# First MLP: the first product of six token tiles as Strassen's seven block products, in pairs

## The chip, the cores and the metric

The kernel runs on one core of one Trainium2 chip. The metric is the device time of one execution in microseconds (us). Three runs of the kernel before gave 1450.2, 1450.25 and 1452.52; their median is 1450.25.

TensorE (PE) does the matrix products, VectorE (DVE) and ScalarE (ACT) everything elementwise. SyncE (SP) issues nearly all DMAs, one after the other. In the trace each engine's instructions run in the order in which the built program has them, with waits on semaphores for the others.

## The reference

Three stages in a row, all in float32. `B, H, S, D = 8, 8, 576, 64`, so there are 4608 tokens of 512 numbers.

```python
kv  = einsum('bhsd,bhse->bhde', k, v)            # linear attention
out = einsum('bhsd,bhde->bhse', q, kv)
out = out / sqrt(mean(out*out, -1) + 1e-6) * g_norm
x   = out.transpose(0, 2, 1, 3).reshape(4608, 512)

h = x @ w_in                                     # first MLP, 512 -> 2048 -> 512
g = s * maximum(h, 0)**2 + b
y = g @ w_out

z = maximum(maximum(y @ w1, y @ w2), y @ w3)     # second MLP, 512 -> 768 -> 512
result = z @ w_out2
```

The two weights of the first MLP and the four of the second arrive as float64 bits, and the kernel turns them into float32 itself.

## The kernel before

**Precision.** Every operand of a product is split into a rounded part (hi) and the rest (lo); a product is three matmuls, hi*hi, hi*lo and lo*hi. `hilo` makes the split with one ACT copy and one DVE subtraction (L92, L93).

**Tiles.** The tokens form 9 tiles of 512. Features lie on the partitions. For one tile the first MLP takes 16 blocks `f` of 128 hidden features. `u1` (L345) makes `h`: 4 parts of the 512 inputs, 3 matmuls each, 12 matmuls of 512 columns. `u1_end` turns `h` into the gates: ACT takes the relu (L354), DVE squares and scales it (L355), ACT adds `b` and rounds it to `gh` (L356), DVE forms the rest `gl` (L357). `u2` (L368) multiplies the gates by `w_out` into four PSUM banks, 12 matmuls again, two blocks behind `u1`. A tile is so 384 matmuls, and each has 12 others between the end of an `h` and the use of its gates.

**Order.** Tiles 0 and 1 share a head in three blocks of hidden features, in which the weights arrive and are turned into float32 (L107 to L112). Tiles 2 to 6 follow one by one, and tiles 7 and 8 share two blocks. Beside tile `t - 1` runs the attention of tile `t`, item by item (an item is two heads of 256 or 320 tokens): `s2` splits `q` on ACT and DVE, `s3` (L266) multiplies it with `kv` on PE, ACT squares the result and scales it (L268, L273), `hilo` splits the square, `s4` (L303, L304) averages it on PE, then ACT takes logarithm, exponential and square (L306 to L308), and DVE corrects and multiplies (L309, L310, L313). `put_x` splits the result into the tile that `u1` reads. From 257 us on a tile takes 96 us, attention included.

**Second MLP.** It runs over pairs of tiles (`SUPERS`) and uses Strassen's scheme in Winograd's form: `combine` forms 7 blocks out of four weight blocks, `tok_steps` 7 out of four token blocks, and `v1` (L508) makes 7 block products where 8 would be the plain way. Its weights are prepared beside the first MLP (`Plain` beside tiles 2 to 6, `combine` and `split_out` beside the last two) and pass through DRAM.

**What decides the order.** The kernel is written as one stream of operations with lists of side work, of which a share is put out after each step of the main work. A scheduler then places the instructions of each engine by the stream's order and its own estimate of when each is ready. The trace has them in that order.

Of the kernel before, what the change touches and what calls it, by code (L numbers as in the profile page):

```python
# [8 lines left out]
F32 = mybir.dt.float32  # L9
# [15 lines left out]
def fused_kernel(ctx, tc, qt, kv, kvr, g_norm, w_in, w_out, s, b, w1, w2, w3, w_out2, out):  # L25
# [17 lines left out]
    XO = 192  # L43
    LIMITS = [CUTS[0]] + [(i + 1) * TW for i in range(NTILE)]

    FA = KF // 2
# [5 lines left out]

    mlp1, attn, low = (ctx.enter_context(ExitStack()) for _ in range(3))
# [3 lines left out]
    wpa = pool("wpa", 2 * FA, st=low, side="right")  # L57
    rawp = pool("rawp", 2, st=mlp1)
    wtp = pool("wtp", 2, st=mlp1)
    wt1 = pool("wt1", 2, st=mlp1)  # L60
    xp = pool("xp", 2, st=mlp1)
    gp = pool("gp", 2, st=mlp1)
    stp = pool("stp", 4, st=mlp1)
    gp1 = pool("gp1", 1, st=mlp1)
    wpb = pool("wpb", 2 * (KF - FA), st=mlp1)
    ps_y = pool("ps_y", 1, PSUM, st=mlp1)
    ps_h = pool("ps_h", 2, PSUM, st=mlp1)
    ps_a = pool("ps_a", 2, PSUM, st=mlp1)
# [7 lines left out]
    start = [wpb.tile([P, NP + 2, P], F32, tag="w", name=f"start{i}") for i in range(EARLY)]  # L76
# [5 lines left out]
    y_dr = [dram.tile([P, KD, TW], F32, name=f"y_dr{t}") for t in range(NTILE)]  # L82
    NQ = KM // 2 * 3
    HW = DM // 2
    wf_dr = [[dram.tile([P, DM], F32, name=f"wf_dr{j}_{m}") for m in range(KM)] for j in range(4)]
# [3 lines left out]
    dma = nc.sync.dma_start  # L89

# [5 lines left out]
    def w_load(src):  # L96
        raw = rawp.tile([P, 2 * DM], U32, tag="raw", name="raw")
        dma(out=raw, in_=src)
        return raw

    def w_float(raw):
        words = raw.rearrange("p (c z) -> p c z", z=2)
        low, high = words[:, :, 0], words[:, :, 1]
        ta = wt1.tile([P, DM], U32, tag="ta", name="ta")
        tb = wtp.tile([P, DM], U32, tag="tb", name="tb")
        af, bf = ta.bitcast(F32), tb.bitcast(F32)
# [6 lines left out]
        return bf  # L113

    def w_parts(bf, nm, f):
        t = (wpa if f < FA else wpb).tile([P, 2, DM], F32R, tag="w", name=nm)
        with tc.high_priority(60):
            hilo(t[:, 0, :], t[:, 1, :], bf)
        return t

    class Weights:
# [6 lines left out]
        def load(self, cnt):  # L128
            while self.loaded < min(cnt, len(self.need)):
                self.raw[self.loaded] = w_load(self.need[self.loaded][0])  # L130
                self.loaded += 1

        def to(self, cnt):
            cnt = min(cnt, len(self.need))
            while self.done < cnt:
                self.load(self.half + 3)
                if self.half < len(self.need):
                    self.f32[self.half] = w_float(self.raw.pop(self.half))
                    self.half += 1
                if self.done < self.half - 1 or self.half == len(self.need):  # L140
                    _, d, key = self.need[self.done]
                    d[key] = w_parts(self.f32.pop(self.done), f"w{self.done}", key)
# [11 lines left out]
    def load_kv(bb, p):  # L154
# [8 lines left out]
        t = wpa.tile([P, NC, 2, P], F32, tag="w", name="kv")  # L163
# [695 lines left out]
```

## Time and profile before

| | |
|---|---|
| runs, us | 1450.2, 1450.25, 1452.52 |
| profiled execution, span, us | 1450.1 |
| PE busy | 1416.9 us, 98% |
| PE weight loads (PEld) busy | 1172.9 us, 81% |
| DVE busy | 893.5 us, 62% |
| ACT busy | 615.6 us, 42% |
| chain that ended last, by engine | PE 82%, DMA 8%, DVE 5%, ACT 3% |
| granted TensorE clock, mean | 0.996 |
| moved by DMA | 217.77 MB, mean 150 GB/s |

The profiled execution has no time of its own but its span, first to last instruction; the fastest run is 0.1 us above it. Busy time is a union: two instructions of one engine that overlap count once, and a matmul that is drawn out by a wait counts as busy.

### The profile page before, as it was taken

Reading aid. Unit: us, or ns where it says so; the run is one execution under the profiler, and the core shown is the slowest. Engines: PE = TensorE matmul, PEld = TensorE weight load, DVE = VectorE, ACT = ScalarE, POOL = GpSimd, SP = SyncE. Lnnn points to the kernel's source line nnn. Section 1 sums busy time; section 2 is a strip of 40 time slices with the busy share of each in tenths; the row PEclk is TensorE's granted clock in tenths of the full one; section 3 lists DMA queues with packets and bytes.
Section 4 is the critical chain, followed back from the end, with each engine's and each line's share of the span. In section 5 each row is a group of like instructions: output and inputs, shape, how many; then the busy total and the mean of one; then the engine's idle time right before and its main releaser. Section 6 shows DMA issues by size and latency. Waiting matters only on the chain.

```text
span 1450.1 us, 18876 instructions
## 1 busy us (share of the span) xinstructions
PE 1416.9 (98%) x7010; PEld 1172.9 (81%) x7010; DVE 893.5 (62%) x1686; ACT 615.6 (42%) x1239; POOL 12.4 (1%) x41
## 2 busy tenths in 40 slices
PE   6899989999999999999999999999999999999998
PEld 4678777888888888888888888888888888888887
DVE  6999999874444454454546656666564573673561
ACT  5764457454454455455544443332232241232221
POOL 1000000000000000000000000000000000000000
PEclk9999999999999999999999999999999999999999
DMA  6665575731111202111013788996553553552521
GB/s 211 182 204 183 163 231 185 231 108 37 44 51 41 73 24 68 41 47 45 14 49 139 238 311 301 360 342 234 185 197 141 185 211 126 187 196 83 186 95 58
DMA packets 67132, 217.77 MB, mean 150 GB/s; under 512 B 8032, under 2 KB 20320, under 8 KB 61280
## 3 DMA queue, kind: packets, MB, share of 16 engines
q1 hardware_dynamic: 66592, 216.56, 43.7%
q8 instruction: 55, 0.90, 0.3%
q14 instruction: 37, 0.30, 0.1%
q10 hardware_dynamic: 448, 0.00, 0.0%
HBM read 165.41 MB, written 51.12 MB: 149 GB/s over the span
## 4 chain that ended last, share of the span: by engine, by line
PE 82%; DMA 8%; DVE 5%; ACT 3%; issue 1%; SPq 0%; POOL 0%; ACTq 0%; DVEq 0%; POOLq 0%
PE h L345 22%; PE y L368 21%; PE r L508 14%; PE x L508 11%; PE o L577 10%; DMA raw<-in_w_out 2%; DMA raw<-in_w 1%; PE kvps L226 1%; PE ops L266 1%; DMA F<-wf_dr 1%; DMA kv<-in_kv 1%; DMA raw<-in_w_in 1%; DVE tb L110 1%; PE mps L226 1%; DMA wc<-wc_dr 1%
## 5 line engine op out<-in xcount | busy, mean ns | idle before, releaser
L345 PE MATMUL h<-xh,w 128*128 128x512 f32 (+1 forms) x1176 | 385.9, 389 | 3.5 <-ACT xh L92 2.2
L368 PE MATMUL y<-gh,w 128*128 128x512 f32 (+1 forms) x1176 | 382.9, 387 | 2.6 <-DVE st L374 1.6
L345 PEld LDWEIGHTS h<-xh,w 128*128 128x128 f32 x1176 | 219.9, 188 | 50.2 <-ACT xh L92 4.7
L368 PEld LDWEIGHTS y<-gh,w 128*128 128x128 f32 x1176 | 220.4, 188 | 48.0 <-ACT gh L356 2.4
L345 PE MATMUL h<-xl,w 128*128 128x512 f32 (+1 forms) x588 | 228.1, 388 | 0.2 <-DVE xl L93 0.2
L368 PE MATMUL y<-gl,w 128*128 128x512 f32 (+1 forms) x588 | 227.4, 387 | 0.1
L357 DVE SCALAR_TENSOR_TENSOR gl<-r,cst,gh 128x512 fp32r<-128x512 f32 (+1 forms) x147 | 108.7, 740 | 121.8 <-ACT gh L356 120.8
L355 DVE SCALAR_TENSOR_TENSOR r<-r,cst 128x512 f32<-128x512 f32 (+1 forms) x147 | 108.7, 739 | 119.4 <-ACT r L354 119.0
L516 ACT ACTIVATE s<-x 128x512 f32<-128x512 f32 (+1 forms) x135 | 74.9, 555 | 236.4 <-PE x L508 235.2
L356 ACT ACTIVATE gh<-r,cst 128x512 fp32r<-128x512 f32 (+1 forms) x147 | 104.9, 714 | 153.7 <-PE y L368 137.4
L354 ACT ACTIVATE r<-h 128x512 f32<-128x512 f32 (+1 forms) x147 | 86.5, 589 | 153.8 <-PE h L345 139.2
L577 PE MATMUL o<-wo,hh 128*128 128x512 f32 x432 | 132.7, 389 | 0.0
L521 DVE TENSOR_TENSOR c<-r,s 128x512 f32<-128x512 f32 (+1 forms) x135 | 81.8, 634 | 82.3 <-ACT s L516 81.2
L345 PEld LDWEIGHTS h<-xl,w 128*128 128x128 f32 x588 | 110.8, 189 | 21.6 <-DVE xl L93 1.1
L368 PEld LDWEIGHTS y<-gl,w 128*128 128x128 f32 x588 | 110.9, 189 | 21.2 <-DVE gl L357 0.3
L577 PEld LDWEIGHTS o<-wo,hh 128*128 128x128 f32 x432 | 80.8, 188 | 16.9 <-ACT hh L92 0.2
L577 PE MATMUL o<-wo,hl 128*128 128x512 f32 x216 | 83.6, 389 | 0.0
L521 DVE TENSOR_TENSOR u<-r,s 128x512 f32<-128x512 f32 (+1 forms) x45 | 28.7, 637 | 65.7 <-PE r L508 65.5
L107 ACT ACTIVATE ta<-raw 128x512 f32<-128x512 f32 x56 | 37.6, 672 | 52.4 <-DMA raw<-in_w_out 23.0
L508 PE MATMUL r<-b21h,wc 128*128 128x512 f32 x144 | 50.3, 389 | 0.0
L508 PE MATMUL r<-b22h,wc 128*128 128x512 f32 x144 | 50.2, 389 | 0.0
L508 PE MATMUL x<-t2h,wc 128*128 128x512 f32 x144 | 50.2, 389 | 0.0
(139 smaller groups left out, 2049.3 us busy)
## 6 DMA issues: line engine op xcount, KB each, us to landing
wc<-wc_dr SPq DMA_DIRECT2D x45, 1792.0 KB, 7.4
kv<-in_kv SPq DMA_DIRECT2D x32, 512.0 KB, 5.6
y_dr<-st SPq DMA_DIRECT2D x56, 256.0 KB, 3.3
raw<-in_w_out SPq DMA_DIRECT2D x22, 512.0 KB, 3.9
raw<-in_w SPq DMA_DIRECT2D x18, 512.0 KB, 3.7
out<-e SPq DMA_DIRECT2D x36, 256.0 KB, 2.0
raw<-in_w_in SPq DMA_DIRECT2D x16, 512.0 KB, 3.7
y<-y_dr SPq DMA_DIRECT2D x32, 256.0 KB, 5.0
```

The costliest lines, as they stand in the source:

```text
L107: nc.scalar.activation(out=af, in_=high.bitcast(F32), func=ACTF.Abs)
L226: last_pe[0] = nc.tensor.matmul(*args, **kw).ins
L345: nc.tensor.matmul(h[:, :n], lhsT=w[:, z, kk, :], rhs=x[:, kk, o:o + n], start=(i == 0), stop=(i == 3 * KD - 1))
L354: nc.scalar.activation(out=rn, in_=h[:, :n], func=ACTF.Relu)
L355: nc.vector.scalar_tensor_tensor(out=rn, in0=rn, scalar=sb_sb[:, 0:1], in1=rn, op0=ALU.mult, op1=ALU.mult)
L356: nc.scalar.activation(out=gh[:, :n], in_=rn, func=ACTF.Identity, bias=sb_sb[:, 1:2])
L357: nc.vector.scalar_tensor_tensor(out=gl[:, :n], in0=rn, scalar=sb_sb[:, 1:2], in1=gh[:, :n].bitcast(F32), op0=ALU.add, op1=ALU.subtract)
L368: nc.tensor.matmul(yt[t, o][j][:, :n], lhsT=w[:, z, c], rhs=r[:, :n], start=(f == fa and i == 0), stop=(f == fb - 1 and i == 2))
L508: nc.tensor.matmul(ps, lhsT=w[:, z, POS[c], kk * P:(kk + 1) * P], rhs=x, start=(first and i == 0), stop=(i == 3 * KD // 2 - 1), skip_group ...
L516: nc.scalar.activation(out=t, in_=ps, func=ACTF.Copy)
L521: nc.vector.tensor_tensor(out=o, in0=ps, in1=t, op=ALU.add)
L577: nc.tensor.matmul(acc[b], lhsT=l[:, o:o + P], rhs=wob[m][:, z, :], start=(m == 0 and i == 0), stop=(m == KM - 1 and i == 2))
```

## The change

Tile 0 and 1 keep their head. Tile 2 now makes all its 16 `h` blocks first: `u1` of the 16 blocks back to back, the squared relu of 14 of them is stored to DRAM (`g_dr`), and of the last two stays. Then `Second` makes the second product of that tile alone: it loads the squares back (`gb`), makes `gh` and `gl` of them (`gate`), and runs 16 times 12 matmuls.

Tiles 3 to 8 form the pairs (3, 4), (5, 6), (7, 8). For a pair, `h_steps` makes two hidden blocks of both tiles by 7 products of 6 matmuls, 8 times. The first tile's gates are used eight products later, in the places `fill`; the second tile's squares go to DRAM and come back in `Second` after the pair's products. So each pair has 336 + 192 + 192 matmuls of 512 columns, where two tiles had 768.

The token blocks of a pair are formed by `tok_steps`, which the second MLP already used; for this the attention writes its result to DRAM (`x_dr`), and `put_x` serves only tiles 0 to 2. The seven weight blocks are formed once (`pair_op`) from float32 weights that went to DRAM (`wi_dr`), used directly by the first pair, and reloaded by the other two (`wp_dr`). The attention of a pair runs beside the tiles before it (`rare_steps`), with an `s4` two places behind its `s3`; in the pairs it has one PSUM bank instead of two. Stores are put out some ticks later than they are asked for (`store`). The weights of the second MLP are prepared from the first pair's `Second` on, beside the second and third pair.

```diff
+    EDGE = 3
+    PAIRS = [(t, t + 1) for t in range(EDGE, NTILE, 2)]
...
+        for a, e in cuts(g0, k, n):
+            o = (g0 + a) % TW
+            store(x_dr[(g0 + a) // TW][:, p, o:o + e - a], og[:, a:e])
...
+    def h_steps(w, T, tb, q, gates):
...
+        def p1():
+            got["x"] = x_bank()
+            prod(w, T, got["x"], A11, "b11", True, False)
+            got["a"] = copy(h_bank("a"), got["x"])
+        def p7():
+            got["d"] = h_bank("d")
+            prod(w, T, got["d"], S3, "t3", True, False)
+            got["p7"] = copy(fpool("p7"), got["d"])
+        def p6():
+            prod(w, T, got["x"], S2, "t2", False, False)
+            got["u2"] = copy(fpool("u2"), got["x"])
+        def p2():
+            a = got.pop("a")
+            prod(w, T, a, A12, "b21", False, False)
+            r = fpool("r")
+            squared(r, a)
+            gates[fa] = gate(r)
+        def p4():
+            d, r = got.pop("d"), fpool("r")
+            prod(w, T, d, A22, "t4", False, False)
+            nc.vector.tensor_tensor(out=r, in0=d, in1=got.pop("u2"), op=ALU.add)
+            squared(r, r)
+            gates[fb] = gate(r)
+        def p5():
+            x, r = got.pop("x"), fpool("r")
+            prod(w, T, x, S1, "t1", False, False)
+            got["b"] = copy(h_bank("b"), x)
+            nc.vector.tensor_tensor(out=r, in0=x, in1=got.pop("p7"), op=ALU.add)
+            squared(r, r)
+            keep(fb, r)
+        def p3():
+            b, r = got.pop("b"), fpool("r")
+            prod(w, T, b, S4, "b22", False, False)
+            squared(r, b)
+            keep(fa, r)
+        return [p1, p7, p6, p2, p4, p5, p3]
...
+    def rare_steps(mine, limit):
...
+            if i:
+                seq += [lambda it=mine[i - 1]: s3(it), rest, lambda it=mine[i - 1]: s4(it, limit)]
...
+        def run(self):
+            self.fetch(4)
+            for k, f in enumerate(self.order):
+                for j in range(KD):
+                    if j == 1:
+                        self.fetch(k + 5)
+                        self.ready(k + 3)
+                    y_mm(self.t, 0, TW, f, j, self.gates[f], k == 0, k == KF - 1)
...
+    for s, (ta, tb) in enumerate(PAIRS):
+        gates = {}
+        if s + 1 < len(PAIRS):
+            beside_of(rare_steps(*groups[5 + s]), 0, V + U - 10)
...
+        after = Second(tb, list(range(KF)), {})
+        for q in range(QF):
+            w = wcs.pop(q)
...
+            order = (0, 0, 2, 0, 2, 0, 4) if fill else (0,) * 7
+            for k, step in enumerate(h_steps(w, toks[s], tb, q, gates)):
+                for _ in range(order[k]):
+                    fill.pop(0)()
+                    tick(3)
+                step()
...
+        nxt = x_of(s + 1) if s + 1 < len(PAIRS) else y_of(0)
+        beside_of(nxt, 10, U - 24)
...
+        after.run()
```

What stands on an engine in a row shows best at two places. On PE before, around an attention item of the middle tiles: `ops` is `s3`, `mps` is `s4`, `h` is `u1`, `y` is `u2`.

```order
L266 MATMUL ops<-ql,kvbd 128x256
L266 MATMUL ops<-qh,kvbd 128x256
L345 MATMUL h<-xh,w_1829 128x512
L345 MATMUL h<-xl,w_1829 128x512
L345 MATMUL h<-xh,w_1829 128x512 x2
L345 MATMUL h<-xl,w_1829 128x512
L345 MATMUL h<-xh,w_1829 128x512 x2
L345 MATMUL h<-xl,w_1829 128x512
L345 MATMUL h<-xh,w_1829 128x512 x2
L345 MATMUL h<-xl,w_1829 128x512
L345 MATMUL h<-xh,w_1829 128x512
L303 MATMUL mps<-sh,ones 128x256
```

Between the item's `s3` and its `s4` stand 12 matmuls of 512 columns. On PE now, in the last products of the first pair: `b`, `x`, `d` are the PSUM banks of `p3`, `p1`, `p7`, and a row with x3 is half of a product.

```order
L288 MATMUL ops<-qh,kvbd 128x256
L288 MATMUL ops<-ql,kvbd 128x256
L288 MATMUL ops<-qh,kvbd 128x256
L587 MATMUL x<-b_3717,wc 128x512 x3
L587 MATMUL x<-b_3828,wc 128x512 x3
L332 MATMUL mps<-sh,ones 128x256
L587 MATMUL d<-t_3807,wc 128x512 x3
L587 MATMUL d<-t_3878,wc 128x512 x3
L333 MATMUL mps<-sl,ones 128x256
```

Here 6 matmuls stand between `s3` and the first matmul of `s4`, and 6 more before its second.

On DVE before, at the border of two middle tiles: squares and gates (L355, L357), and between them the attention (L93, L309 to L313).

```order
L357 SCALAR_TENSOR_TENSOR gl<-r,cst,gh 128x512
L93 TENSOR_TENSOR xl<-og,xh 128x320
L355 SCALAR_TENSOR_TENSOR r<-r,cst 128x512
L93 TENSOR_TENSOR ql<-qt,qh 128x320
L93 TENSOR_TENSOR sl<-sq,sh 128x320
L357 SCALAR_TENSOR_TENSOR gl<-r,cst,gh 128x512
L355 SCALAR_TENSOR_TENSOR r<-r,cst 128x512
L309 SCALAR_TENSOR_TENSOR t<-mps,t 128x320
L310 SCALAR_TENSOR_TENSOR t<-t,y_6348 128x320
L313 TENSOR_TENSOR og<-og,t 128x320
```

Between two gates stand four instructions. On DVE now, between tile 2's last three gates (`gl<-gb`) and the first pair: `b_` and `t_` are token blocks, L564 is their additions, L430 copies a result out of PSUM.

```order
L115 TENSOR_TENSOR b_3828<-y_3778,b_3828 128x512
L115 TENSOR_TENSOR b_3834<-y_3796,b_3834 128x512
L405 SCALAR_TENSOR_TENSOR gl<-gb,cst,gh 128x512
L564 TENSOR_TENSOR y_3778<-y_3802,y_3778 128x512
L564 TENSOR_TENSOR y_3802<-y_3813,y_3802 128x512
L115 TENSOR_TENSOR b_3840<-y_3813,b_3840 128x512
L115 TENSOR_TENSOR t_3862<-y_3778,t_3862 128x512
L564 TENSOR_TENSOR y_3813<-y_3813,y_3778 128x512
L430 COPY st<-y_3370 128x512
L564 TENSOR_TENSOR y_3796<-y_3796,y_3813 128x512
L115 TENSOR_TENSOR t_3868<-y_3813,t_3868 128x512
L115 TENSOR_TENSOR t_3878<-y_3802,t_3878 128x512
```

The token blocks of the first pair are formed here in one run, with one gate between them where four instructions stood between two gates. The first row, `b_3828`, is what the first product needs last; the last row, `t_3878`, is what the second product needs last, ten instructions behind it.

## Rows read from the trace of the kernel before

**Rows 1.** The page, busy time, share of the span and count by engine.

```profile
PE 1416.9 (98%) x7010; PEld 1172.9 (81%) x7010; DVE 893.5 (62%) x1686; ACT 615.6 (42%) x1239; POOL 12.4 (1%) x41
```

**Rows 2.** Stretches: start:end, us, busy us (count) by engine, clock, DMA share, GB/s.

```profile
200.00:260.00 60.00, 54.33 (x279) 42.93 (x277) 56.09 (x130) 40.89 (x95) 0.75 (x2) 1.00 0.68 218
300.00:700.00 400.00, 400.00 (x2094) 332.78 (x2093) 198.70 (x381) 197.30 (x425) 4.30 (x14) 1.00 0.15 48
750.00:900.00 150.00, 150.00 (x667) 124.29 (x666) 91.57 (x156) 66.81 (x111) 0.00 (x0) 1.00 0.64 226
900.00:975.00 75.00, 71.88 (x485) 65.57 (x484) 50.65 (x113) 25.73 (x59) 0.00 (x0) 1.00 0.93 353
```

**Rows 3.** The chain that ended last: start us, us, what; its last piece.

```profile
1413.82 32.65 PE o L577 x144
```

**Rows 4.** Waits of PE from 200 to 260 us: total us, times, longest.

```profile
PE mps L303 <- ACT sh L92: 3.0, 2, 2.6
PE mps L304 <- DVE sl L93: 1.5, 3, 1.2
```

**Rows 5.** Order of time, 205 to 211 us: start, us, what, [idle before <-releaser].

```profile
205.05 1.89 DVE L374 TENSOR_TENSOR st<-st,y 128x512 f32<-128x512 f32 x3
...
205.48 0.28 PE L266 MATMUL ops<-qh,kvbd 128*128 128x256 f32 x1
...
207.69 0.60 ACT L354 ACTIVATE r<-h 128x512 f32<-128x512 f32 x1 [1.05 <-DVE gl L357]
...
208.49 0.38 ACT L268 ACTIVATE sq<-ops 128x256 f32<-128x256 f32 x1
...
210.59 0.41 ACT L92 ACTIVATE sh<-sq 128x256 fp32r<-128x256 f32 x1
...
211.05 0.38 PE L303 MATMUL mps<-sh,ones 128*128 128x256 f32 x1 [2.56 <-ACT sh L92]
```

**Rows 6.** Order of time, 615 to 618 us, same columns.

```profile
615.29 0.28 PE L266 MATMUL ops<-qh,kvbd 128*128 128x256 f32 x1
...
616.82 0.41 ACT L92 ACTIVATE sh<-sq 128x256 fp32r<-128x256 f32 x1
...
617.26 0.42 DVE L93 TENSOR_TENSOR sl<-sq,sh 128x256 fp32r<-128x256 f32 x1 [0.16 <-ACT sh L92]
...
618.16 0.28 PE L303 MATMUL mps<-sh,ones 128*128 128x256 f32 x1
```

**Rows 7.** Order of time, 1111 to 1114 us, second MLP, same columns.

```profile
1111.25 1.29 DVE L521 TENSOR_TENSOR c<-r,s 128x512 f32<-128x512 f32 x2 [1.91 <-ACT s L516]
...
1112.86 0.39 PE L508 MATMUL x<-b11h,wc 128*128 128x512 f32 x1
...
1113.29 0.60 ACT L516 ACTIVATE s<-x 128x512 f32<-128x512 f32 x1 [2.07 <-PE x L508]
...
1114.44 0.39 PE L508 MATMUL x<-t2h,wc 128*128 128x512 f32 x1
```

**Rows 8.** Groups of DVE by shape, 300 to 900 us: count | busy us, mean ns | idle.

```profile
L355 DVE SCALAR_TENSOR_TENSOR r<-r,cst 128x512 f32<-128x512 f32 x104 | 78.1, 751 | 118.1 <-ACT r L354 117.9
...
L93 DVE TENSOR_TENSOR wlo<-F,whi 128x1024 fp32r<-128x1024 f32 x9 | 11.0, 1224 | 2.4 <-ACT whi L92 2.0
...
L310 DVE SCALAR_TENSOR_TENSOR t<-t,y 128x256 f32<-128x256 f32 x20 | 8.5, 425 | 0.6
```

**Rows 9.** Groups of ACT by shape, 300 to 900 us.

```profile
L356 ACT ACTIVATE gh<-r,cst 128x512 fp32r<-128x512 f32 x103 | 74.6, 724 | 138.1 <-PE y L368 131.4 <-DVE r L355 4.5 <-PE mps L304 2.2
L354 ACT ACTIVATE r<-h 128x512 f32<-128x512 f32 x104 | 62.3, 599 | 142.6 <-PE h L345 135.2 <-DVE gl L357 7.4
L307 ACT ACTIVATE y<-y,cst 128x320 f32<-128x320 f32 x19 | 10.7, 563 | 0.6
```

**Rows 10.** DMA issues: count, KB each, median us from issue to landing.

```profile
wc<-wc_dr SPq DMA_DIRECT2D x45, 1792.0 KB, 7.4
...
y<-y_dr SPq DMA_DIRECT2D x32, 256.0 KB, 5.0
```

More of the change, by code (lines that the diff above doesn't have):

```diff
@@ L89, in fused_kernel, with store, stores_due @@
     dma = nc.sync.dma_start
+    clock = [None]
+    waiting = []
+    def store(out, in_, n=9):
+        if clock[0] is None:
+            dma(out=out, in_=in_)
+        else:
+            waiting.append((clock[0] + n, out, in_))
+            waiting.sort(key=lambda e: e[0])
+    def stores_due(now):
+        while waiting and waiting[0][0] <= now:
+            _, o, i = waiting.pop(0)
+            dma(out=o, in_=i)
     def hilo(hi, lo, src):
@@ L361, in u2, with y_mm @@
+    def u1_end(h, n):
+        r = gp1.tile([P, TW], F32, tag="g", name="r")[:, :n]
+        squared(r, h[:, :n])
+        return gate(r)
+    def y_mm(t, o, n, f, j, g, first, last):
         gh, gl = g
         if (t, o) not in yt:
[L363 to L364 removed]
+            yt[t, o] = {}
+        if j not in yt[t, o]:
+            yt[t, o][j] = ps_y.tile([P, TW], F32, tag=f"y{j}", name=f"y{j}")
+        c = slice(j * P, (j + 1) * P)
+        for i, (z, r) in enumerate(((0, gh), (0, gl), (1, gh))):
+            nc.tensor.matmul(yt[t, o][j][:, :n], lhsT=wo[f][:, z, c], rhs=r, start=(first and i == 0), stop=(last and i == 2))
@@ new lines, in tok_steps, with prod, x_bank, h_bank @@
+        return seq
+    def prod(w, T, bank, c, nm, first, alone=True):
+        i = 0
+        for kk in range(KD // 2):
+            hi, lo = T[nm, kk]
+            for z, x in ((0, hi), (0, lo), (1, hi)):
+                nc.tensor.matmul(bank, lhsT=w[:, z, POS[c], kk * P:(kk + 1) * P], rhs=x, start=(first and i == 0), stop=(i == 3 * KD // 2 - 1), skip_group_check=not alone)
+                i += 1
+    def h_steps(w, T, tb, q, gates):
+        got = {}
+        fa, fb = 2 * q, 2 * q + 1
+        def x_bank():
+            return ps["x"].tile([P, TW], F32, tag="x", name="x")
+        def h_bank(nm):
+            return ps_h.tile([P, TW], F32, tag="h", name=nm)
+        def copy(out, bank):
+            nc.scalar.activation(out=out, in_=bank, func=ACTF.Copy)
+            return out
+        def keep(f, r):
+            store(g_dr[tb][f], r)
+        def p1():
[34 more added lines that the diff above has]
+        return [p1, p7, p6, p2, p4, p5, p3]
@@ new lines, in all_beside @@
+    def all_beside():
+        for s in sides:
+            for fn in s[0][s[1]:]:
+                fn()
+        sides.clear()
+        stores_due(math.inf)
+    ONE = 3 * KD
+    clock[0] = 0
+    flush_held()
+    t = EDGE - 1
+    direct = {}
+    beside_of(rare_steps(*groups[4]), 0, 24 * ONE)
+    for f in range(KF):
+        h = u1(t, 0, TW, f)
+        if pend:
+            u2(*pend.pop(0))
+        r = stage()
+        squared(r, h)
+        if f < KF - 2:
+            store(g_dr[t][f], r)
+        else:
+            direct[f] = gate(r)
+        tick(ONE)
```

583 lines of the change are left out of this document (352 added, 231 removed).

## The prediction

> **What bounds the kernel now.** I read the page's busy shares first, then the stretches, then the chain's last piece, then single waits. PE is busy for 1416.9 of 1450.1 us, no other engine over 62% [rows 1]. From 300 to 900 us PE's busy time is the whole stretch, while DVE and ACT stand at about half of 300 to 700 us, and the granted clock is 1.00, the 2.4 GHz level [rows 2]. Busy is not yet fast, so I take PE's pace from a run without any wait: 144 matmuls of 512 columns in 32.65 us, 0.2268 us each [rows 3]. A tile's 384 matmuls are then 87.1 us of its 96, and the attention beside it has the rest. There the kernel can only gain by fewer matmuls.
>
> There are two places where PE does wait. From 200 to 260 us, with DVE busy for 93% and ACT for 68%, it is idle 5.7 us [rows 2], most of it in front of `s4` [rows 4]. The longest of these waits shows how: the last matmul of `s3` starts at 205.48, ACT comes to its square only at 208.49, since the relu before it waited for DVE, which had three additions of a result to do; the split of the square starts at 210.59, and PE has stood 2.56 us [rows 5]. In the middle tiles the same chain runs from 615.29 to 617.23 for the hi part and to 617.68 for the lo part, and PE asks at 618.16 [rows 6]. The second place is the start of the second MLP, where weights of 1792 KB come at 353 GB/s [rows 2]; it stays as it is.
>
> **What goes.** Counted in the built programs, `h` of the first MLP takes 1692 matmuls of 512 columns before; now it takes 540 there and 1008 in the block products. That is 144 fewer, 48 for each pair. At 0.2268 us: **32.7 us less**. Everything else on PE keeps its count: second products, attention, second MLP.
>
> The Trainium skill, "TensorE: Matmul & The Clock Gate", section "Back-to-back issue gap", has a sustained 131 ns for matmuls of 512 columns with their weight loads, and about 216 ns for an isolated one. By the first the 144 would be worth 18.9 us, by the second 31.1; the trace's 227 ns speaks against the first, and the sums here use the 227.
>
> **What the other engines get, and where it hides.** Take eighths of the first pair's products (66 matmuls of 512 columns, 15.0 us, and two attention items, about 1.5 us). ACT has 4 copies out of PSUM at 0.60, as the second MLP's [rows 7], 4 relus at 0.60 and 2 gates at 0.72 [rows 9]; each of the two items has 7 instructions of 0.38 to 0.56 us, here taken as 0.45 [rows 5, 9]; a weight pair in three of four eighths rounds 1792 columns, 2.1 us at 0.60 for 512. Sum 6.2 + 6.3 + 1.6 = 14.1 us. DVE has 6 squares and gates at 0.75 and 2 additions at 0.69, two items of 5 instructions at about 0.46, and in three of four eighths 4 short additions at 0.42 and 1792 columns of subtraction at 1.22 per 1024 [rows 8]: 5.9 + 4.6 + 2.9 = 13.4. But neighbours on an engine overlap: three additions take 1.89 and two 1.29 [rows 5, 7], so one more costs 0.60, and one alone the 0.69 used here: about 0.09 goes from each. With that both engines come to some 12 us of 16.5, near 75%. In tile 2's second product DVE has 14 gates, two weight pairs and the token blocks, 22 instructions of 512 columns, on top of the attention: about 40 us of 53. So neither becomes the bound, but both stand between the quiet 50% and the crowded 93% of [rows 2], and what counts is how long a chain through them takes.
>
> **Attention.** This is the largest cost I see: behind an `s4` that waits, all other matmuls queue. From tile 2 on 40 items stand in the new order; before, at least 12 matmuls (2.7 us) lay between `s3` and `s4`. Now 6 items have 5 or 6 (1.1 to 1.4 us), 8 have 8 or 9 (1.8 to 2.0), 3 have 10 (2.3), 9 have 12, 13 have 15 to 18, and one has none. From the start of the next matmul after `s3` the quiet chain needs 1.8 us to the hi part and 2.3 to the lo part [rows 6]. So even at quiet pace the first six lose about 0.7 each and the next eight 0.1: 5 us. At the crowded pace of 5.4 us [rows 5] the 28 items up to the end of the first pair lose some 3 each: 85 us. Both ends stay for the range. At 75% I take a chain 0.5 longer than the quiet one, since that load is nearer to the quiet row: the groups lose 1.2, 0.6, 0.4 and 0.2 each, 7.2 + 4.8 + 1.2 + 1.8 = **15 us more**.
>
> **Turnover of the PSUM banks.** A product cannot go on in a bank before the copy out of it is done. In the second MLP the last matmul into `x` starts at 1112.86 and ends at 1113.25, the copy runs from 1113.29 to 1113.89, and the bank's next matmul starts at 1114.44, six matmuls behind [rows 7]: 0.55 us of room. In the pairs the shortest distance is the same, six matmuls: the relu of `p3` has `p1` as cover before `p7` needs the bank. Behind `p1` and `p5` there are 12 and more; their copies write into PSUM instead of SBUF, which no row here shows, and would stay covered at twice the 0.60. At ACT's half-full pace this costs nothing; when ACT is inside the rounding of 1024 weight columns, 1.2 us at the same rate, the room is exceeded by some 0.5. With one such meeting in two eighths, 24 eighths cost 24 x 0.2 = **5 us**, between 0 and 24 x 1.0. The first eighth of each pair has no second products between its steps, or only a few: the copy behind `p5` then stands open, 0.7 us each: **2 us**.
>
> **Through DRAM.** Tile 2's squares come back by loads that begin when its last `h` has read its tokens; two gates are kept, 24 matmuls or 5.4 us of cover. A 256 KB load lands after 5.0 us [rows 10] and the hi part takes 0.72 [rows 9]: 5.7 us, so a wait of 0.3, and 3 if it lands as late as the 7.4 us of the large loads. Later loads run four blocks ahead, and the pairs' first three are asked for before the pair ends: hidden. A load has SP's queue to pass, where stores wait for their data; those are put out late for this, and if one still stands in front, its wait adds to the load. The token blocks of the first pair end only about when its first product could start (DVE's row in the section on the change): with 11 instructions of 0.6 us behind the last block of the first product and 24 matmuls to go, it fits, with less than 2 us to spare. Together **2 us**, from 0 to 10.
>
> **What comes back.** Between 200 and 260 us DVE now has no float conversion of the second MLP's weights. The 4.5 us of waits in front of `s4` there [rows 4] should mostly go: **4 us less**. In return 16 float weights are stored in the head, 256 KB each; a buffer is written again two weights later, and the loads behind these stores wait longer for their own buffer. I count nothing, at most 5 us.
>
> **Sum.** 1450.1 - 32.7 + 15 + 5 + 2 + 2 - 4 = 1437.4, against the profiled span, and the median of the runs is 0.15 above that. I say **1437 us**.
>
> **Rivals.**
> 1. *The cover holds.* The order of the new program was laid by readiness, and the quiet chain needs only 5 us for all items; the banks cost nothing and the start 1: 1450.1 - 32.7 + 5 + 2 + 1 - 4 = 1421. For it: in [rows 6] PE asks half a microsecond after the lo part is there, and the second MLP runs this scheme without waits at the bank. Against it: both rows have engines half empty.
> 2. *Attention becomes the bound* (slower). If `s3` to `s4` takes 3.4 us for the hi part and 4.0 for the lo part, as it takes when ACT's in-order queue holds a relu that waits for DVE, the 27 items under 2.8 us lose about 1.5 each, and banks and start go to their upper halves: 40 + 10 + 4 = 54, less 4 and 32.7: 1467. It decides from a chain of about 3 us on. For it: [rows 5]; one bank for all attention in the pairs, so that the next `s3` waits for the whole of `s4`. Against it: DVE at 75% and not 93%.
> 3. *The gain is eaten exactly.* Chains of about 2.8 us and late token blocks at each of three pairs: 30 us, 1448 to 1453.
>
> That the change doesn't save the matmuls is excluded, since the built program holds 144 fewer.
>
> **Chances.** The forecast, 1427 to 1447: 0.53. The cover holds, under 1427: 0.24. Eaten, 1447.3 to 1453.2: 0.08. Slower: 0.15. A difference under 0.2%, about 3 us, is what a measurement of this kernel can't tell from none. So faster 0.77, same 0.08, slower 0.15. Range 1416 to 1458.
>
> **What would show it.** In the new profile the waits of PE from tile 2 to the end of the first pair: in front of `mps`, on ACT's `sh` or DVE's `sl`, some 15 us, and little of it in the second pair, whose items have 15 to 18 matmuls. A wait on a copy (`a`, `b`) or on `r` in front of a product `d`: some 5 us, more in the first pair than in the third, which has no attention. At 227 ns per matmul elsewhere, and a granted clock of 1.00, all is as said. The third pair's products should take 504 matmuls or 114 us and little more. Wrong would be: waits on `gb` or on token blocks that repeat at each pair, a clock under 1.00 in a pair, or a head that is longer than 257 us by the new stores.

## The result and the profile after

Four runs of the changed kernel gave 1428.45 to 1430.34 us, median **1429.26**. The kernel before, beside them, had a median of 1451.38. The ratio is 0.9852, 95% interval 0.9833 to 0.9871: 22 us faster. The forecast was 1437, with a range of 1416 to 1458. The profiled execution has a span of 1428.1 us.

The page's line of the engines, which answers to [rows 1]:

```profile
PE 1392.1 (97%) x6866; PEld 1146.4 (80%) x6866; DVE 963.3 (67%) x1768; ACT 684.7 (48%) x1337; POOL 12.9 (1%) x41
```

PE has 144 instructions fewer and 24.8 us less busy time; DVE and ACT have some 70 us more each. The pace of a matmul is what it was: the chain's last piece has the same length as in [rows 3].

```profile
1391.69 32.65 PE o L727 x144
```

The stretches, with the columns of [rows 2]: the head's end, the first and second pair with the changes between them, the third pair's start, and the second MLP's start.

```profile
200.00:260.00 60.00, 58.45 (x298) 46.95 (x297) 37.07 (x75) 34.43 (x83) 0.61 (x2) 1.00 0.39 126
310.00:440.00 130.00, 129.53 (x685) 104.81 (x685) 100.09 (x186) 93.83 (x193) 1.84 (x6) 1.00 0.68 239
490.00:620.00 130.00, 129.94 (x650) 106.80 (x649) 96.12 (x179) 78.32 (x152) 1.14 (x2) 1.00 0.72 244
670.00:790.00 120.00, 117.78 (x516) 96.22 (x515) 91.74 (x156) 64.73 (x104) 0.00 (x0) 1.00 0.89 316
...
880.00:900.00 20.00, 15.71 (x107) 15.00 (x107) 11.12 (x25) 6.67 (x15) 0.00 (x0) 0.83 0.99 364
900.00:955.00 55.00, 54.41 (x361) 49.47 (x360) 32.83 (x80) 17.43 (x41) 0.00 (x0) 1.00 0.83 310
```

In the first pair DVE is busy for 77% and ACT for 72%, as forecast, and still PE hardly stands. The one of these stretches with a low clock, 880 to 900 us, is one that the forecast had left as it was. The waits of PE from 237 to 900 us (total us, times, longest), where [rows 4] had those in front of `s4` (L332 and L333 are the `s4` of now):

```profile
PE x L587 <- ACT s L667: 4.2, 2, 3.7
PE y L421 <- ACT gh L404: 1.7, 2, 1.5
PE mps L332 <- ACT sh L114: 1.3, 1, 1.3
PE x L587 <- ACT a L602: 0.7, 1, 0.7
PE mps L333 <- DVE sl L115: 0.2, 1, 0.2
```

**Lost time by stage.** For each matmul I took the time from its start to the next one's start, less the pace of a run of its shape (0.2268 us for 512 columns, 0.146 for 320, 0.1175 for 256, 0.035 for the small products of `k` and `v`). What is left is lost, by a wait, a change between instructions or a low clock. Two of the kernels of the section below stand beside it:

| stage, us lost | before | before, conversions held | after | after, loads of the second MLP moved |
|---|---|---|---|---|
| 0 to 100 us | 44.8 | 44.3 | 47.1 | 48.0 |
| 100 to 257.7 | 10.6 | 2.3 | 5.7 | 4.7 |
| 257.7 to the second MLP | 3.5 | 3.4 | 12.5 | 12.7 |
| its first 70 to 75 us | 6.6 | 4.8 | 10.8 | 3.3 |
| the rest | -0.2 | -0.2 | -0.3 | -0.3 |
| sum | 65.3 | 54.6 | 75.8 | 68.4 |

With 32.7 us of matmuls gone and 10.5 more lost, the span should be 22.2 us shorter; it is 22.0. The limits between the first stages are times and not places in the program, so work can cross them; each column is one execution.

**An attention item now**, order of time from 289 us, one of those with few matmuls between `s3` (L288) and `s4`; it answers to [rows 6].

```profile
289.41 0.28 PE L288 MATMUL ops<-qh,kvbd 128*128 128x256 f32 x1
...
289.53 0.40 PE L376 MATMUL h<-xh,w 128*128 128x512 f32 x1
...
289.87 0.38 ACT L290 ACTIVATE sq<-ops 128x256 f32<-128x256 f32 x1
...
290.13 0.48 ACT L295 ACTIVATE og<-ops,cst 128x256 f32<-128x256 f32 x1
...
290.49 0.43 ACT L114 ACTIVATE sh<-sq 128x256 fp32r<-128x256 f32 x1
...
290.94 0.43 DVE L115 TENSOR_TENSOR sl<-sq,sh 128x256 fp32r<-128x256 f32 x1 [0.19 <-ACT sh L114]
...
290.96 0.38 PE L332 MATMUL mps<-sh,ones 128*128 128x256 f32 x1
...
291.43 0.38 PE L333 MATMUL mps<-sl,ones 128*128 128x256 f32 x1
```

ACT takes `sq` 0.18 us after `s3` has ended, then `og` and `sh` at once. From the start of the next matmul after `s3` the hi part is there after 1.39 us and the lo part after 1.84; in [rows 6] these were 1.8 and 2.3, and the forecast had added 0.5 to them. Both `s4` matmuls start 0.04 and 0.06 us after their operand is ready: the order fits without a gap. Over the 40 items from tile 2 on, the median time from the end of `s3` to the end of `sh` is 1.30 us; over the 38 items in the same part of before it was 1.8.

**Where a gate came late**, order of time at 677 us, in the second product of tile 6.

```profile
677.19 0.39 PE L421 MATMUL y<-gh,w 128*128 128x512 f32 x1
...
677.57 0.84 ACT L114 ACTIVATE hl<-F 128x768 fp32r<-128x768 f32 x1 [4.14 <-DMA F<-wf_dr]
...
678.32 0.71 ACT L404 ACTIVATE gh<-gb,cst 128x512 fp32r<-128x512 f32 x1
...
679.08 1.21 PE L421 MATMUL y<-gh,w 128*128 128x512 f32 x4 [1.50 <-ACT gh L404]
```

ACT had stood for 4.14 us on the rounding of weights whose load had not landed, and the gate was next in its queue. The same happens at the second MLP's start, order of time from 882 us; here it is the larger loss.

```profile
878.22 2.26 SPq L111 DMA_DIRECT2D y_dr<-st  x4
...
880.53 1.90 SPq L552 DMA_DIRECT2D y<-y_dr  x4
...
882.93 0.88 PE L587 MATMUL r<-t,wc 128*128 128x256 f32 x6
...
885.95 1.27 ACT L114 ACTIVATE b<-y 128x512 fp32r<-128x512 f32 x2 [4.60 <-DMA y<-y_dr]
...
887.13 0.36 ACT L667 ACTIVATE s<-x 128x256 f32<-128x256 f32 x1
...
887.55 1.65 PE L587 MATMUL x<-t,wc 128*128 128x256 f32 x6 [3.73 <-ACT s L667]
```

SP issues the token loads of the next group (`y<-y_dr`) only behind the last four stores. ACT's split of them stands in its queue ahead of the copy `s<-x`, waits 4.60 us for the load, and PE waits 3.73 us for the copy. Then six matmuls take 1.65 us where six of the same shape took 0.88 before the pause: the clock is down to 1.2 GHz.

### The profile page after: what moved, and what is told of

It reads as the page before. It is cut to its first block, busy times and chain, and to the rows that moved or that the text cites. A ratio compares the mean times of both kernels' runs of the same rounds, so it can differ in the third digit from the quotient of the medians.

```text
span 1428.1 us, 19202 instructions
## 1 busy us (share of the span) xinstructions
PE 1392.1 (97%) x6866; PEld 1146.4 (80%) x6866; DVE 963.3 (67%) x1768; ACT 684.7 (48%) x1337; POOL 12.9 (1%) x41
## 4 chain that ended last, share of the span: by engine, by line
PE 84%; DVE 6%; DMA 5%; ACT 3%; issue 1%; SPq 0%; POOL 0%; ACTq 0%; DVEq 0%; POOLq 0%
PE y L421 21%; PE x L587 18%; PE r L587 15%; PE o L727 10%; PE h L376 6%; PE d L587 4%; PE a L587 2%; PE b L587 2%; DMA raw<-in_w_out 1%; PE ops L288 1%; PE kvps L248 1%; DMA raw<-in_w_in 1%; DMA wf_dr<-tab 1%; PE mps L248 1%; DVE r L393 1%
## 5 line engine op out<-in xcount | busy, mean ns | idle before, releaser
L587 PE MATMUL x<-t,wc 128*128 128x512 f32 (+1 forms) x828 | 201.1, 378 | 4.4 <-ACT s L667 3.7
L587 PEld LDWEIGHTS x<-t,wc 128*128 128x128 f32 x828 | 149.1, 189 | 33.1 <-ACT s L667 3.9
L376 PE MATMUL h<-xh,w 128*128 128x512 f32 (+1 forms) x408 | 135.2, 390 | 3.6 <-ACT xh L114 3.1
L587 PE MATMUL r<-b,wc 128*128 128x512 f32 (+1 forms) x540 | 127.0, 371 | 0.1
L587 PE MATMUL r<-t,wc 128*128 128x512 f32 (+1 forms) x540 | 118.8, 368 | 0.0
L587 PEld LDWEIGHTS r<-b,wc 128*128 128x128 f32 x540 | 96.6, 191 | 17.6 <-DVE u L705 0.3
L587 PEld LDWEIGHTS r<-t,wc 128*128 128x128 f32 x540 | 95.0, 189 | 16.8
L587 PE MATMUL x<-b,wc 128*128 128x512 f32 (+1 forms) x414 | 100.7, 379 | 0.7 <-ACT s L667 0.7
L376 PEld LDWEIGHTS h<-xh,w 128*128 128x128 f32 x408 | 77.0, 192 | 20.4 <-ACT xh L114 5.5
L376 PE MATMUL h<-xl,w 128*128 128x512 f32 (+1 forms) x204 | 79.4, 389 | 0.2
```

What stands on the lines that cost most here:

```text
L376: nc.tensor.matmul(h[:, :n], lhsT=w[:, z, kk, :], rhs=x[:, kk, o:o + n], start=(i == 0), stop=(i == 3 * KD - 1))
L587: nc.tensor.matmul(bank, lhsT=w[:, z, POS[c], kk * P:(kk + 1) * P], rhs=x, start=(first and i == 0), stop=(i == 3 * KD // 2 - 1), skip_gro ...
```

## Experiments

**1. Are the matmuls the bound?** `p7` is made twice, the second time into the same bank: 144 matmuls more.

```diff
             prod(w, T, got["d"], S3, "t3", True, False)
+            prod(w, T, got["d"], S3, "t3", True, False)
```

> The new kernel, with the product p7 of every eighth made twice into the same bank (the second overwrites the first): 144 matmuls of 512 columns more, nothing else. Theory A: PE is the bound all through the pairs, so each matmul costs its full 0.2268 us: 32.7 us more, 1462 (1460 to 1464). Rival B: in the pairs the chains through ACT and DVE set part of the pace, and the added matmuls are partly absorbed as cover: 10 to 25 us more, 1439 to 1454.

Measured 1460.1 (ratio to before 1.007, 1.0051 to 1.009): 30.8 more than the changed kernel, and 34.3 more between the profiled spans (the profile is of the slowest of its four runs). The 32.7 of the forecast lies between. PE's pace is the bound of the pairs, so the matmuls taken away were worth their full time, as far as these runs can tell.

**2. Do the banks need more room?** The eight fills of each eighth all stand before `p3`, so that six matmuls are the only cover everywhere else.

```diff
-            order = (0, 0, 2, 0, 2, 0, 4) if fill else (0,) * 7
+            order = (0, 0, 0, 0, 0, 0, 8) if fill else (0,) * 7
```

> The new kernel, with all eight second products of an eighth put in front of p3, instead of two before p6, two before p4 and four before p3. Between p1 and p6 then lie six matmuls instead of twelve. Theory A: a bank turns over in 0.64 us, six matmuls (1.36 us) cover it, also at 75% load: 1429 (1427 to 1431). Rival B, the prediction's term: with six matmuls a copy that finds ACT busy is late by half a microsecond every few times; now at three places of each eighth instead of one: 5 to 15 us more, 1434 to 1444.

Measured 1430.38 (0.986, 0.9844 to 0.9875), the time of the changed kernel. Six matmuls cover the turnover at the load of the pairs; the 5 us of the forecast were not there.

**3. Does the load of ACT and DVE lengthen the attention's chain?** The items beside the first two pairs are squeezed into two thirds of the ticks.

```diff
-            beside_of(rare_steps(*groups[5 + s]), 0, V + U - 10)
+            beside_of(rare_steps(*groups[5 + s]), 0, (V + U - 10) * 2 // 3)
```

> The changed kernel with the attention beside the first and second pair squeezed into two thirds of the ticks, so that the load of ACT and DVE there rises by about a third of the attention's share (some 10% of the stretch) and the shared bank comes free later for the next item. Theory A (the order is laid by what the scheduler reckons the chains to take, and ACT and DVE have room): within 3 us of 1429.3. Theory B (the forecast's reading, the chain through ACT and DVE lengthens with their load): PE waits in front of s4 by 5 us and more, 1434 to 1445.

Measured 1433.88 (0.9882, 0.9866 to 0.9898), 2 to 5 us more than the two measurements of the changed kernel: between the two expectations, and the reason is neither's. The waits in front of `s4` stay at 1.5 us in all, and the median from `s3` to `sh` is 1.25 us. What is new is a wait of 1.3 us in front of an `s3`, for the product of `k` and `v`. The load rose by much less than expected: in 310 to 440 us ACT went from 72 to 76% and DVE from 77 to 78%, in 490 to 620 us ACT from 60 to 62%, and DVE fell from 74 to 72%. So this run does not say what a higher load would do. It does say something of the cover: 18 of the 40 items now have 6 matmuls between `s3` and `s4`, where 5 had, and still `s4` does not wait.

**4. What if the chain is longer all the same?** Three more ACT copies of the square stand between `s3` and its split.

```diff
+        if clock[0] is not None:
+            for _ in range(3):
+                nc.scalar.activation(out=sq, in_=sq, func=ACTF.Copy)
         sh, sl = temps(it, "sh"), temps(it, "sl")
```

> The changed kernel, with three more ACT copies of each attention item's square between s3 and its split, from tile 2 on (40 items): about 0.42 us each, so the chain from s3 to s4 grows by 1.26 us. Theory A (the order is laid by the chain that the scheduler reckons with, so its cover grows with the chain; in the built order the matmuls between s3 and s4 go from about 2 us to about 4 for most items): the time stays within 3 us of the changed kernel's 1429, waits in front of s4 stay under 5 us. Theory B (the forecast's rule, a longer chain against the cover that stands in the changed kernel's trace: 35 items would be late, by 31 us together): 1455 to 1462.

Measured 1447.28 (0.9969, 0.9954 to 0.9984): 18 us more than the changed kernel. The median from `s3` to `sh` is now 3.4 us, just where the second rival of the forecast decides. But the waits in front of `s4` are 0.7 us in all, since the order was laid anew, and the 18 us stand elsewhere. The largest piece behind the head and ahead of the second MLP is at 314 us, order of time (SPq is SP's DMA queue):

```profile
312.16 1.04 SPq L965 DMA_DIRECT2D gb<-g_dr  x2
...
314.41 0.38 ACT L290 ACTIVATE sq<-ops 128x256 f32<-128x256 f32 x1 [2.26 <-PE ops L288]
314.58 0.59 SPq L111 DMA_DIRECT2D x_dr<-og  x1
...
315.22 0.92 SPq L965 DMA_DIRECT2D gb<-g_dr  x2
...
315.66 0.86 ACT L298 ACTIVATE sq<-sq 128x256 f32<-128x256 f32 x2
...
317.69 0.72 ACT L407 ACTIVATE gh<-gb,cst 128x512 fp32r<-128x512 f32 x1 [1.17 <-DMA gb<-g_dr]
...
318.46 0.73 PE L424 MATMUL y<-gh,w 128*128 128x512 f32 x2 [4.09 <-ACT gh L407]
...
320.80 0.63 PE L424 MATMUL y<-gh,w 128*128 128x512 f32 x1
...
321.23 0.63 PE L424 MATMUL y<-gl,w 128*128 128x512 f32 x1
```

PE waits 4.09 us for a gate (`gh`). On ACT that gate stands behind the item's `sq` and `og` and all three added copies, which end at 316.52; the time up to there is ACT's own queue. Then ACT waits another 1.17 us for the gate's squares: the attention's result is later, so SP's store of it waits for its data till 314.58, and the loads of squares stand behind it. When PE goes on, its matmuls soon start 0.43 us apart, till 322.9, which adds 1.8 us. The granted clock of this stretch:

```profile
314.00:324.00 10.00, 5.91 (x21) 4.68 (x21) 4.21 (x9) 6.47 (x14) 0.00 (x0) 0.83 0.97 339
```

A second piece, at 517 us, is the one bank that the attention has in the pairs. `s3` waits until DVE has read the `s4` before it:

```profile
514.68 0.39 PE L336 MATMUL mps<-sl,ones 128*128 128x256 f32 x1
...
517.08 0.42 PE L288 MATMUL ops<-qh,kvbd 128*128 128x320 f32 x1 [2.01 <-DVE t L341]
```

The remaining waits are of the first kind: a relu that PE waits 1.8 us for at 257 us stands on ACT behind the item's first added copy, and the wait for the copy `a` is 1.4 us instead of 0.7. So neither theory: the scheduler's cover follows the chain, as the first says, but the three copies also stand in ACT's queue ahead of gates and relus that PE needs, and a later result holds SP's queue and the bank; those are paid. The edit made ACT busier as well as the chain longer, so it does not price the chain alone.

**5. What were the weight conversions worth?** First I let the preparation of the second MLP's weights in the kernel before start one tile later.

```diff
-    early = next(i for i, sl in enumerate(slots) if sl[0] == HEAD)
+    early = next(i for i, sl in enumerate(slots) if sl[0] == HEAD + 1)
```

> The kernel before, with the float conversion of the second MLP's weights beginning one tile later (beside tile 3 instead of tile 2, from where the scheduler had drawn it forward into 180 to 260 us). Theory A: this conversion crowded DVE and cost PE the waits before 260 us, so part of the change's gain is not Strassen's: 1443 to 1446. Rival B: the waits come from the order of the attention there and stay: 1449 to 1452.

Measured 1449.7 (0.9998, 0.9988 to 1.0009). This says nothing on the question: in the built order the conversions stand at the same places on ACT and DVE as before (14 start on ACT between 180 and 260 us before, 13 here); I take it that the scheduler draws them forward as soon as their buffers are free. So I tied each one behind the latest relu and square of the main work (`main["dve"]` is the square, kept in the same way):

```diff
-        nc.scalar.activation(out=rn, in_=h[:, :n], func=ACTF.Relu)
+        main["act"] = nc.scalar.activation(out=rn, in_=h[:, :n], func=ACTF.Relu).ins
...
             if self.done < len(self.need):
-                dma(out=self.need[self.done][1], in_=w_float(self.raw.pop(0)))
+                with tc.issue_after(main["act"]), tc.issue_after(main["dve"]):
+                    tab = w_float(self.raw.pop(0))
+                dma(out=self.need[self.done][1], in_=tab)
```

> The kernel before, with each float conversion of the second MLP's weights held behind the main work's latest relu and square in the order of ACT and DVE, so that none stands in the head any more (in the built order the first held one lies at the start of tile 2). Theory A (relief): these conversions made DVE late between 200 and 258 us; without them DVE's busy share from 200 to 260 us falls from 93% to under 80%, the waits in front of s4 there fall from 4.5 us to under 1.5, and the kernel takes 1442 to 1447, 4 to 9 us less than before. Theory B: the gain of the changed kernel in this stretch comes from something else (its pools, its order); then 1449 to 1451, with the waits as they were. Theory C: the conversions crowd the middle tiles instead and the loss moves there: 1449 or more, with the waits in front of s4 gone before 258 us and new ones behind it.

Measured 1442.02 (0.9938, 0.9924 to 0.9952): **9 us less than before with not one matmul fewer.** The stretch of [rows 2] in this kernel:

```profile
200.00:260.00 60.00, 59.99 (x305) 48.70 (x304) 39.69 (x85) 36.95 (x88) 0.62 (x2) 1.00 0.33 107
```

PE is busy for all of it, where it had 54.33; DVE went from 56.09 to 39.69. The waits of [rows 4] are gone, and nothing new comes in the middle tiles (3.4 us lost there, 3.5 before). The conversions' loads and stores left the stretch with them (the DMA share is 0.33, where it was 0.68), but what PE had waited for there were ACT's and DVE's splits. The table above shows 8.3 us less lost between 100 and 257.7.

**6. What do the stores in the head cost?** The kernel before, with the 16 stores of the float weights; nothing reads them.

```diff
                     self.f32[self.half] = w_float(self.raw.pop(self.half))
+                    _, d, key = self.need[self.half]
+                    if d is wi:
+                        dma(out=wi_dr[key], in_=self.f32[self.half])
```

> The kernel before, with 16 stores of 256 KB in the head, each float weight of the first product to DRAM, as the changed kernel has them; nothing reads them. Theory A: these stores are what made the first 100 us of the changed kernel lose 2.3 us more than before: 1452 to 1454. Theory B: the stores are hidden, and the difference there is of the order of the head's instructions: 1449.5 to 1451.5.

Measured 1453.92 (1.0021, 1.0013 to 1.003): they cost some 3 us in the kernel before. But not where the first theory has them. In this kernel's trace the first 100 us lose 42.0 us, less than before, and 100 to 257.7 us lose 17.1 instead of 10.6: by longer waits for `sh` and for an addition of results, and by matmuls at the lower clock (granted 0.91 from 200 to 260 us, against 1.00). The traced execution is the slowest of the 11. So the 2.3 us more in the first 100 us of the changed kernel are not explained by it. The nine traces with the changed kernel's head and its stores on SP lose 46.0 to 48.7 us there, the three with the head of before and no stores (before and both edits of experiment 5) lose 43.6 to 44.8.

Up to the first matmul of tile 2, with the same matmuls in front of it in every kernel, the trace takes 245.7 us before, 236.3 with the conversions held, 249.7 with the stores, and 240.4 in the changed kernel. In sum the two edits (9.4 less and 4.0 more) would make the 5.3 less of the changed kernel, though they do not stand at the same places.

**7. The second MLP's start.** The token loads that come late there are put out 14 to 26 ticks before the last pair ends:

```diff
+        if s + 1 == len(PAIRS):
+            early_y = y_of(1)
+            beside_of(early_y[:4], U - 26, U - 14)
...
-    nxt = y_of(1)
-    for fn in nxt[:4]:
-        fn()
+    nxt = early_y
```

> The new kernel, with the first four token loads of the second MLP's second pair put out some 20 matmuls before the last second product ends, instead of behind the last result stores. Theory A: at the start of the second MLP ACT stands in line behind a split whose token load landed late (PE waits 3.7 us for a copy, then runs 4 us at the lower clock); with the loads early the loss of 10.8 us from 880 to 955 us falls to about 3, the time to 1422 (1420 to 1424). Rival B: the weights, 1792 KB each, set the pace there as before the change; the copy waits less but PE waits for them instead: 1427 to 1430.

Measured 1425.28 (0.9827, 0.9811 to 0.9843), 4 us less than the changed kernel: between the two expectations. The wait for the copy is 0.2 us now, but another comes in its place:

```profile
PE r L587 <- DMA wc<-wc_dr: 2.4, 1, 2.4
```

A weight pair of 1792 KB comes behind six loads of `w_out2`. I moved these from the start to the fourth to ninth product set:

```diff
-    for m in range(KM):
-        wob[m] = wop.tile([P, 2, DM], F32R, tag="wo", name="wo2")
-        dma(out=wob[m].bitcast(F32), in_=wo_dr[m])
...
             wm_load(si * NQ + q + 3)
+            if si == 0 and q >= 3:
+                m = q - 3
+                wob[m] = wop.tile([P, 2, DM], F32R, tag="wo", name="wo2")
+                dma(out=wob[m].bitcast(F32), in_=wo_dr[m])
```

> The changed kernel with the second MLP's second token loads issued earlier, as in the earlier experiment that took 1425.3, and with the six loads of w_out2 (512 KB each) moved from the start of the second MLP to its fourth to ninth product set, so that they no longer stand ahead of its weights in the DMA queue. Theory A (the 2.4 us wait of PE for a weight pair there is queueing behind these 3 MB, 8 us at 360 GB/s): that wait goes, 1422 to 1424. Theory B (the stretch is bound by the rate of the DMA as such, so the wait comes at another place): 1425 to 1427.

Measured 1425.37 (0.9827, 0.9809 to 0.9846). The wait moved to `w_out2`:

```profile
PE o L727 <- DMA wo<-wo_dr: 3.0, 1, 3.0
```

Then one of them behind each of the first six sets (`q < KM` in place of `q >= 3`, `m = q`):

> The changed kernel with the earlier token loads, and the six loads of w_out2 spread over the first six product sets of the second MLP, one behind each weight load, where they stood all at the start (then PE waited 2.4 us for a weight pair) or behind the fourth to ninth set (then it waited 3.0 us for w_out2). Theory A (the wait is a matter of order in the DMA queue, since 900 to 955 us leaves a fifth of it idle): both waits under 1 us, 1421.5 to 1424. Theory B (the stretch moves a fixed number of bytes at the DMA's rate, wherever they stand): one of the two waits stays, 1424.5 to 1426.5.

Measured **1423.12** (0.9811, 0.9797 to 0.9826), the best of all. Both waits are gone, and the stretches of this kernel show PE running at the full clock:

```profile
880.00:900.00 20.00, 19.83 (x162) 19.38 (x161) 11.43 (x30) 5.75 (x16) 0.00 (x0) 1.00 1.01 393
900.00:955.00 55.00, 54.80 (x339) 48.98 (x338) 30.07 (x70) 16.12 (x36) 0.00 (x0) 1.00 0.80 305
```

So it was the order in the queue, not the bytes: the waits show it, while the time alone can't be told from the 1425.28 of the first version, since the intervals overlap. Beside it the changed kernel ran once more:

> The changed kernel once more, beside the version above on the same chip, so that a few us between the two can be told: 1428.5 to 1430.5.

It took 1431.55 (0.9867, 0.9851 to 0.9884), 8 us more than the version with both sets of loads moved. It is also 1.2 us above the highest of the first four runs, so a difference of 2 us between single kernels is not to be trusted here. Its trace loses 3 us more than the first one between tile 2 and the second MLP: the wait at 677 us is 1.86 us instead of 1.50, with 1.8 us lost to the lower clock behind it, and the rest is in small pieces.

**8. The head's stores through another queue.** With the early token loads kept, the 16 stores go out by POOL's queue:

```diff
-                        dma(out=wi_dr[key], in_=self.f32[self.half])
+                        nc.gpsimd.dma_start(out=wi_dr[key], in_=self.f32[self.half])
```

> The kernel with the earlier token loads (1425.3), and the 16 stores of the head put out by POOL's queue instead of SP's. Theory A (the stores cost the head some 3 us because they stand in SP's queue until their data is there, with loads of weights and keys behind them): 1421.5 to 1423.5, and the loss of the first 100 us falls to that of the kernel before. Theory B (they cost by their bytes and by the buffers that wait for their landing): 1424.5 to 1426.5.

Measured 1428.36 (0.9855, 0.9832 to 0.9878), some 3 us worse than with SP, with intervals that overlap by little. So taking the stores out of SP's queue does not save what they cost; whether POOL's queue brings a cost of its own was not tried. The first 100 us lose 48.8 here, against 46.2 with SP; what the stores cost by, bytes, buffers or the order of the head's work, stays open.

## Why the prediction was right, and where not

The direction, the bound and the range held; the size was 8 us too pessimistic. It was 9.3 by spans (1437.4 against 1428.1): the sum started from a span, and every run is 1.7 to 1.9 us longer than the span of its core, which it did not add. The costs of the pairs were put 15 us too high and two other places, the head and the second MLP's start, 6.5 us too low, so part of the closeness is luck.

| term | forecast | measured |
|---|---|---|
| 144 matmuls | -32.7 | 28.6 to 30.8 for 144 more, by runs; 34.3 by spans |
| attention, banks, first eighths, through DRAM | +24 | +9.0 (12.5 - 3.5); 3 more in the repeated run |
| relief from 100 to 257.7 us | -4 | -4.9 (5.7 - 10.6) |
| stores in the head | 0, at most 5 | +2.3 in the first 100 us, its cause open; 4.0 in experiment 6, behind them |
| start of the second MLP | 0 | +4.2 (10.8 - 6.6) |
| sum | -12.7 | -22.1 |

**The step that failed** is "at 75% I take a chain 0.5 longer than the quiet one". The load was right (72 and 77%). But the chain became 0.5 us shorter. What sets it is the place of `sq` in ACT's order: in the item of [rows 6] a gate and a split of `q` stand ahead of `sq`, now it comes right behind `s3`. ACT in that item, from the trace of before (order of time):

```profile
615.26 0.73 ACT L356 ACTIVATE gh<-r,cst 128x512 fp32r<-128x512 f32 x1 [1.93 <-PE y L368]
615.89 0.40 ACT L92 ACTIVATE qh<-qt 128x256 fp32r<-128x256 f32 x1
616.20 0.36 ACT L268 ACTIVATE sq<-ops 128x256 f32<-128x256 f32 x1
```

`s3` ends there at 615.57, so `sq` starts 0.63 us behind it, where it was 0.18 above; that is the difference of the two items' chains. Load and chain are not tied as I had it: at 72 and 77% the median is 1.30 us, and at the half-full load of the middle tiles before it was 1.8. The term was 15 us; PE waits 1.3 us in front of an `s4` once, at 256 us, where no matmul stands between it and its `s3`, an item that the sum had left at nothing, and 0.2 us in all behind that.

**Counting the matmuls as cover** was a second error of that step. I set a chain of my own against the cover in the built order, as if the two had nothing to do with each other. In experiment 4 the cover grew with the chain, from a median of 12 matmuls (2.7 us) to 17 (3.9 us) over the 40 items. The scheduler puts `s4` where it reckons the split to be ready; the cover is short where it reckons the chain short, and here, as in experiment 3 with its six matmuls, it was right.

**The second rival's mechanism** was not met, but its other half, one bank for all attention, is what experiment 4 shows at 517 us. Its condition, a chain of 3.4 us, cost 18 us there and not 40, and hardly any of it in front of `s4`.

**Banks and first eighths.** Of 5 + 2 us there is one wait, 0.7 us for the copy `a` behind `p1` in the third pair's first eighth: the size I gave for the copy behind `p5`, while the one behind `p1` was to be covered. Between 714.71 and 830.38 us the third pair's 504 matmuls take 115.7 us; 114.3 would be at pace.

**Through DRAM.** The loads of squares land after 5.0 us, as [rows 10] had for that size. No load was late for PE directly. The one wait of 1.5 us comes through ACT's queue, from a load that has nothing to do with the squares. I had looked for this on SP only.

**What the 9.0 are.** 1.5 is the wait at 677 us and 0.7 that for the copy `a`. One more piece, 1.2 us at 310 us, stands around an `s4` with five matmuls of cover and the gate behind it. The rest is spread over the stretch in some 80 pieces of 0.05 to 0.2 us. By the same count, what is lost next to a matmul of the attention is 5.0 us from 257.7 us to the second MLP, and 0.2 before; that this neighbourhood is the cause was not tried.

**Relief.** Right in sum, by two sizes that offset each other. The conversions alone were worth 8.3 us there (experiment 5), and the changed kernel gives 3.4 of it back, 1.1 at 158 us and 1.8 at the `s4` without cover. So 9 us, of the 22 that the change brings, can be had without the seven products: against the kernel before with its conversions held, the change brings 1442.0 - 1429.3 = 12.7 us out of 32.7.

**The second MLP's start** I had left as it was, because its weights and rate did not change. But the token loads in front of it did: they now come from the last pair's own stores. The order showed it: on ACT a split that waits for a load stands ahead of the copy that PE needs.

**The first rival**, that the cover holds, with 1421 us, was as far from the measured time as the forecast, but nearer in its mechanism: its costs for these add up to 8 us, and 9.0 were measured. The two places that it did not have either, the head and the second MLP, are most of what keeps the kernel from it. With the loads there moved it runs in 1423.1.

## What to carry to other kernels

Ask first of every wait on an in-order engine what else stands behind it there: here behind the head, the two longest waits of PE came from an instruction on ACT that waited for a DMA and held up another that PE needed. Where a scheduler lays the order, as here, it lays the cover for the chain that it reckons with, so count how the built order places the chain's own instructions, not the load of the engines alone. And before a gain is put down to less work, make the old kernel with its side work moved too: 9 us could be had that way, against 22 by the whole change.

## What the runs showed of the hardware

A pause of PE can cost more than its length, and its length alone does not decide it. After pauses of 3.73 us (the changed kernel at 887 us), 4.09 and 2.01 us (experiment 4 at 318 and 517 us) matmuls come at half the pace, with a granted clock of 0.50, the 1.2 GHz level, for three to six microseconds; this adds 3.3, 1.8 and 1.7 us. The granted clock is 0.83 both in 880 to 900 us and in the stretch of experiment 4 shown above. After the pauses of 1.50 us at 679 us and 1.30 us at 256 us in the changed kernel they come at the full pace; but in its repeated run the pause at 679 us is 1.86 us, and the low clock follows. And the longest wait of [rows 5], 2.56 us up to 211.05 us, is not followed by the low clock, while the wait at the same place in the kernel of experiment 6, 2.54 us up to 211.06 us, is. The two kernels from 210 to 218 us, with the columns of [rows 2], that of before first:

```profile
210.00:218.00 8.00, 6.78 (x32) 5.61 (x33) 6.88 (x15) 5.25 (x13) 0.00 (x0) 1.00 0.77 260
210.00:218.00 8.00, 6.93 (x19) 5.47 (x20) 5.05 (x12) 3.75 (x9) 0.00 (x0) 0.57 0.79 247
```

What else decides stays open here. The 0.43 us between matmuls of 512 columns at the low clock agree with the Trainium skill, "TensorE: Matmul & The Clock Gate", section "Back-to-back issue gap", which gives N / 1.2 ns for the slow level, 427 ns. So the wait of 3.73 us at the second MLP's start was worth about twice its length, 7.0 us with the slow matmuls behind it: without it, and with no other in its place, the stage loses 7.5 us less (10.8 to 3.3, experiment 7).
